# Filters moved within SBUF, and GpSimd's tables at later slots, in a Fourier filter with an MLP behind it

## Chip, core and metric

The kernel runs on one core of one Trainium2 chip. The metric is the device time of one execution in microseconds (us); the kernel before takes 736.68 us, the median of three runs (736.36 to 736.72). Engines are named as in the profile: PE is TensorE's matmul, PEld its weight load, DVE is VectorE, ACT is ScalarE, POOL is GpSimd and SP is SyncE, which here only issues DMAs.

## The reference

Eight batches of 3008 rows and 256 channels go through a global filter in the frequency domain, and each row of the result through a two-layer MLP with an exact GELU:

```python
def _attn_ref(x, filt_r, filt_i):           # x: 8 x 3008 x 256; filters: 1505 x 256
    X = np.fft.rfft(x, axis=1)
    F = (filt_r + 1j * filt_i)[None, :, :]
    return np.fft.irfft(X * F, n=x.shape[1], axis=1)

def _moe_ref(x, w_in, w_out):               # x: 24064 x 256; w_in: 256 x 2048; w_out: 2048 x 256
    h = x @ w_in
    g = 0.5 * h * (1.0 + erf(h / sqrt(2)))
    return g @ w_out
```

The output is 24064 x 256 in float32.

## The kernel before

**The transform.** A batch's 3008 rows are split as 47 x 64, so that the Fourier transform becomes two stages of small matmuls with a table of twiddle factors between them, the product with the filters, and two stages back. For batches 1 to 7 the stages have these names. `fold` (line 102) makes sums and differences of the two halves of x in place, on DVE; `s1` (line 418) is the first stage, in four calls c = 0 to 3 of eight matmuls, whose results DVE and ACT copy out of PSUM into `a_sb` and SP writes to a DRAM buffer R1. `r1` reads that back in another order as `b_sb`. `s2` (line 451) is the second stage, in three units u; `s2_out` multiplies its results by the filters on DVE, and `s2_sum` adds the parts of the complex product (L477, L478). `s3` is the first stage back; its results go through `v_sb` to a DRAM buffer R2, `r2` reads them as `d_sb`, and `s4` is the last stage, which uses the table T4a and writes the ring `y_sb` that the MLP reads. Batch 0 goes through a path of its own (`c1` to `c4`), which uses the filters F as they were loaded.

**The filters.** `F` holds the filters for 24 frequencies k on 64 partitions, loaded in three pieces (k from 0, 4 and 12) by POOL's DMA queue; `dup_filters` copies them to the other 64 partitions. Later batches need the same filters in another order, `Fu`: 128 partitions and six columns m, two for each unit. In the kernel before, `save_filters` writes F to DRAM (16 DMAs on SP), and `load_filters_again` reads it back into Fu, which lies over one half of F: columns m = 0 and 1 by POOL's queue at slot 1, and columns 2 to 5 by SP's at slot 18.

**The tables.** POOL builds what batches 1 to 7 need beside the filters: `table_2_parities` (T2p, read by s2), `table_u_pick` (for `table_u`, which makes the table U that s3 reads), `table_4_rows` and `weights_4` (T1g, T2g and two columns of weights), from which `table_4_factors` makes the factors of T4a with three matmuls and three copies on ACT, and `table_4_all`, which builds T4a of products of these factors in eight parts, two to a call; a part is two products (L414) and a sum (L416). T2, the table that several of these read, shares its buffer with the tile `s_sb` of the MLP.

**The MLP.** Rows are taken in 47 tiles of 512. A tile t has 16 slots, one for each 128 columns of the hidden layer: `mm1` (L643) gives 128 x 512 to a bank of PSUM, ACT applies the GELU (L646) and writes `g_sb`. The second matmul of all tiles but two uses seven products in place of eight (`mm2_seven`, L719), of sums that DVE makes: `sums_1` (L688), `sums_2` (L694) and `sums_3` (L701, into the tile `s4_sb`). Tiles 0 and 2 use the plain product (L659).

**What sets the order.** There is no scheduler: the order of each engine's instructions is the order in which the program is written. A loop runs over slots s = 0 to 767, 16 for each tile; `put(slot, f, ...)` lists a call for a slot, and at each slot the listed calls come first, then this slot's share of the second matmul and its mm1. The calls of batch b + 1 are so spread over the slots of batch b's rows. An instruction waits for what it reads and for the buffer that it writes, and all behind it on its engine or DMA queue waits with it. `gate` (line 143) is a copy of one element on POOL: what is behind it in POOL's queue waits until that element is written. `evac` copies out of PSUM, on ACT when told "act" and on DVE when told False.

Of the kernel before, what the change touches and what calls it, by code (L numbers as in the profile page):

```python
# [20 lines left out]
HB = 32  # L21
# [10 lines left out]
class _Mix:  # L32
    def __init__(self, ctx, tc, x, filt_r, filt_i, w_in, w_out, out):
        self.tc, self.nc = tc, tc.nc
        self.x, self.filt_r, self.filt_i = x, filt_r, filt_i
        self.w_in, self.w_out, self.out = w_in, w_out, out
        self.B, self.S, self.D = x.shape
        self.DFF = w_in.shape[1]
        assert self.S == NA * NB and self.D == 256 and self.DFF == 2048
        pool = lambda name, bufs, **kw: ctx.enter_context(tc.tile_pool(name=name, bufs=bufs, **kw))  # L40
        P = bass.MemoryType.PSUM
        self.const = pool("const", 1)
        self.px = pool("px", 1)
        self.pa = pool("pa", 3)
        self.pb = pool("pb", 2)
        self.pp = pool("pp", 3)
        self.pv = pool("pv", 2)
        self.pd = pool("pd", 3)
        self.pool = pool
        self.po = pool("po", 4)  # L50
        self.py = pool("py", 1)
        self.pg = pool("pg", 2)
        self.pq = pool("pq", 1)
        self.small = pool("small", 1)
        self.dram = pool("dram", 2, space=bass.MemoryType.DRAM)
        c = self.const
        self.T1 = c.tile([2 * NA, 96], BF16, name="T1")
        self.T2p = c.tile([128, K1, 2, 2, 16], BF16, name="T2p")
        self.xs = c.tile([128, 4, 256], BF16, name="xs")
        self.U = c.tile([128, 2, 2 * HB], BF16, name="U")  # L60
        self.T4a = c.tile([96, HB, 96], BF16, name="T4a")
        self.T4c = c.tile([96, NA, 2], BF16, name="T4c")
        self.F = c.tile([128, 2, K1, 256], BF16, name="F")
        self.Fu = self.F[:, 0].rearrange("p (t a m) c -> p t a m c", t=2, a=2)
        self.w_in_sb = c.tile([128, 2, self.DFF], BF16, name="w_in_sb")
        self.w_out_sb = c.tile([128, 16, self.D], FP16, name="w_out_sb")
        self.w_sums = c.tile([128, 4, 8, 128], FP16, name="w_sums")
        self.ps, self.st = {}, {}
        self.flip = 0
# [46 lines left out]
            for q, a in enumerate((direct, mirror)):  # L116
                nc.gpsimd.dma_start(out=self.F[32 * q:32 * q + 32, t, k0:k0 + k, :], in_=a)

    def save_filters(self, k0, k):

        if "Fd" not in self.st:
            self.st["Fd"] = self.dram.tile([2, 2, 4, 2, 16, 6, 256], BF16, tag="Fd", name="Fd")
        for t in range(2):
            for q in range(2):
                for c in range(k0 // 6, (k0 + k) // 6):
                    o = self.st["Fd"][:, t, c, q].rearrange("a i m c -> i a (m c)")
                    if q:
                        o = o[:, ::-1]
                    self.nc.sync.dma_start(out=o, in_=self.F[32 * q:32 * q + 32, t, 6 * c:6 * c + 6, :])

    def load_filters_again(self, eng, m0, m):

        for t in range(2):
            for a in range(2):
                i = self.st["Fd"][a, t, :, :, :, m0:m0 + m, :].rearrange("c q i m d -> (c q i) (m d)")
                eng.dma_start(out=self.Fu[:, t, a, m0:m0 + m, :].rearrange("p m d -> p (m d)"), in_=i)

    def dup_filters(self, eng, k0, k):
        for k in range(k0, k0 + k, 2):
# [278 lines left out]
    def s1(self, b, c):  # L418

        nc = self.nc  # L420
        if c == 0:
            self.st[b, "R1"] = self.dram.tile([NB, 48, 256], BF16, tag="R1", name="R1")
        if b == 1 and c == 3:
            at = self.pp.tile([128, 2, 4, 256], BF16, tag="p12", name="p12").rearrange("p t k c -> p (t k) c")
        else:
            at = self.pa.tile([128, 8, 256], BF16, tag="a", name="a_sb")
        x = self.st[b, "s", c], self.st["x1"][:, 1, 4 * c:4 * c + 4]
        lent = "o" if b == 1 and c < 2 else "h"
        ps = [[self.bank("ps_s1", lent if i == v == 0 else "f") for v in range(2)] for i in range(2)]
        for i in range(2):  # L430
            for d in range(2):
                for v in range(2):
                    nc.tensor.matmul(ps[i][v][64 * d:64 * d + 64, :], lhsT=self.T1s[64 * v:64 * v + NA],  # L433
                                     rhs=x[d][64 * v:64 * v + NA, 2 * i:2 * i + 2, :], start=True, stop=True)
# [59 lines left out]
        self.s3_out(b, u, 0)  # L494

    def s3_out(self, b, u, i):
        vt = self.pv.tile([128, 2, 512], BF16, tag="v", name="v_sb")
        for c in range(2):
            self._evac(vt[:, c], self.st[b, "ps3"][2 * i + c], False if b == u == i == c == 1 else "act")
        for a in range(2):  # L500
            self.nc.sync.dma_start(out=self.st[b, "R2"][:, u, a, 2 * i:2 * i + 2],
                                   in_=vt[64 * a:64 * a + 64].rearrange("p c (m d) -> p c m d", m=2))
# [191 lines left out]
        self.nc.vector.tensor_tensor(out=a21[:, k], in0=self.st["s", t][:, k, 0], in1=a22[:, k], op=ALU.add)  # L694

    def sums_3(self, t, i):
        if i == 0:
            self.st["s4", t] = self.pq.tile([128, 8, 256], FP16, tag="s4", name="s4_sb")
        _, a12, s2, _ = self.quarters(t)
        k = slice(i, i + 4)  # L700
        self.nc.vector.tensor_tensor(out=self.st["s4", t][:, k], in0=a12[:, k], in1=s2[:, k], op=ALU.subtract)  # L701

    def mm2_seven(self, t, lo, hi):

        nc, v = self.nc, self.nc.vector.tensor_tensor
        a11, a12, s2, a22 = self.quarters(t)
        w = self.w_out_sb.rearrange("p (i k) (n o) -> p k n i o", k=2, n=2)
        q = self.w_sums
        s31, s4 = self.st["s", t], self.st.get(("s4", t))
        ops = ((a11, w[:, 0, 0]), (a12, w[:, 1, 0]), (s2, q[:, 1]), (s31[:, :, 0], q[:, 2]),  # L710
               (s31[:, :, 1], q[:, 0]), (a22, q[:, 3]), (s4, w[:, 1, 1]))
        last = t == self.B * self.S // TCH - 1
        for n in range(lo, hi):
# [4 lines left out]
            a, b = ops[m]  # L718
# [69 lines left out]
def kernel(  # L788
# [14 lines left out]
    g = m.small  # L803
# [58 lines left out]
    m.warm_up(1)  # L862
    m.c1t(0, (False, act))
    m.dup_filters(nc.gpsimd, 4, 20)
    for k in (12, 0):
        m.save_filters(k, 12)
    m.c1t(1, (act,))
    m.table_3_copy(1, 0)
    m.c2(0)
# [46 lines left out]
    def put(slot, f, *a):  # L916
        at.setdefault(slot, []).append((f, a))
# [5 lines left out]
    for b in range(1, B):  # L923
        hi = first(b)
        e = 4 * (b == B - 1)
        s1, n1, r1 = (4, 2.75, 16) if b == 1 else (hi - 87, 3.7, hi - 73) if b == 2 else (hi - 94 - e, 3.7, hi - 80 - e)
        s2 = (30, 43, 56) if b == 1 else (hi - 74, hi - 59, hi - 44) if e else (hi - 64 + (b == 2), hi - 48, hi - 32)
        busy.update(range(s1 - 1, s1 + int(3 * n1) + 2))
        for c in range(4):
            slot = s1 + int(c * n1 + (b == 1 and c in (1, 2)))  # L930
            put((0, 1, 5, 8)[c] if b == 1 else (70, 74, 86, 94)[c] if b == 2 else hi - 94 - (20, 13, 8, 6)[c], m.fold, b, c)
            put(slot, m.s1, b, c)
        for u in range(3):
# [16 lines left out]
    for b in range(1, B):  # L950
# [8 lines left out]
        for u in range(7, -1, -1):  # L959
            due = (b * S + GRP * u) // TCH * 16  # L960
            end = min(end, due - 2 if u or b > 1 else 83)
            if b == u == 1:
                end = 85
            for half in (1, 0):
                while end in busy:
                    end -= 1
                assert end > after[b] + 7
                put(end, m.s4, b, u, half, act if half or end in crowd or b == 1 and u == 0 else False)
                busy.add(end)
                end -= 1 if u < 3 else 2  # L970
            if u % 2 == 0:
                put(after[b] if u == 0 else end - 11, m.r2, b, u // 2)

    put(0, m.table_4_rows, g)
    put(0, m.weights_4, g)
    put(0, m.table_u_pick, g)
    put(0, m.table_2_parities)
    put(14, m.table_4_factors, g)
    put(18, m.table_u)
    parts = [(w, h) for w in range(0, HB, 8) for h in range(2)]  # L980
    for i, slot in enumerate((15, 45, 52, 104)):
        put(slot, m.table_4_all, parts[2 * i:2 * i + 2])
    put(1, m.load_filters_again, nc.gpsimd, 0, 2)
    put(18, m.load_filters_again, nc.sync, 2, 4)
    put(20, m.weight_sums)
    plain = (0, 2)
    seven = [t for t in range(NT) if t not in plain]
# [54 lines left out]
```

## Time and profile before

| | us |
|---|---|
| median of three runs | 736.68 |
| the profiled execution | 737.13 |
| its span | 735.3 |
| PE busy in the span | 716.1 |
| first matmul of the MLP (slot 0) | 38.24 |
| first s2 of batch 1 (slot 30) | 62.90 |
| first s4 of batch 1 (slot 82) | 112.67 |

A profile is one execution of the program as the hardware profiler recorded it, with times in us from the start of the span. A line of the timeline gives start, length, engine, source line and operation, the tile written and the tiles read, the shape and how often; brackets at its end hold the time for which the engine was idle before it, and the instruction that ended this. Lines of the windows view give a stretch's length and how long each engine was busy in it. The TensorE clock is at its full rate in every slice of this profile. The start of the span, to 38 us, is batch 0's transform; from there PE works on the MLP with the transforms of the later batches in between.

### The profile page before, as it was taken

The numbers are of one execution on the slowest core, as the hardware profiler recorded it, in microseconds if no ns is written. First come the engines' busy times: TensorE is split into PE (matmuls) and PEld (weight loads), VectorE is DVE, ScalarE is ACT, GpSimd is POOL, SyncE is SP. The second block draws the span as 40 slices with busy tenths as digits, with TensorE's granted clock in tenths as the row PEclk, the third lists the DMA queues.
The fourth block names the chain that finished last, engine by engine and source line by source line (L and its number), as shares of the span: only waits on it lengthen the run. The fifth ranks groups of instructions, "written<-read, shape, count | busy, mean of one in ns | idle before, by whom it ended". The sixth has DMA issues, their size and how long they took to land.

```text
span 735.3 us, 22145 instructions
## 1 busy us (share of the span) xinstructions
PE 716.1 (97%) x9063; PEld 506.5 (69%) x9213; DVE 604.6 (82%) x1105; ACT 575.4 (78%) x1049; POOL 291.2 (40%) x547
## 2 busy tenths in 40 slices
PE   8999999999999999999999999999999999999998
PEld 4856666677777767676677767666677767777776
DVE  8886797899887998789986989779998898675566
ACT  6997677688887888778887788877888788777773
POOL 7895744656122553134621355114631122122121
PEclk9999999999999999999999999999999999999999
DMA  8996435655345643545545455455544433311011
GB/s 145 211 187 213 107 91 116 196 144 110 83 132 172 125 99 105 149 145 117 119 124 171 104 115 124 116 151 132 120 109 127 148 100 102 111 38 52 30 58 59
DMA packets 81190, 89.30 MB, mean 121 GB/s; under 512 B 13201, under 2 KB 60433, under 8 KB 81089
## 3 DMA queue, kind: packets, MB, share of 16 engines
q0 software_dynamic: 22480, 40.02, 23.8%
q1 hardware_dynamic: 58193, 47.66, 23.4%
q8 instruction: 72, 1.18, 0.7%
q14 instruction: 29, 0.24, 0.1%
q10 hardware_dynamic: 416, 0.20, 0.1%
HBM read 55.57 MB, written 48.23 MB: 141 GB/s over the span
## 4 chain that ended last, share of the span: by engine, by line
PE 88%; DVE 3%; DMA 3%; POOL 2%; issue 2%; ACT 1%; DVEq 0%; POOLq 0%
PE ps_o L719 40%; PE ps_h L643 38%; PE ps_s L518 3%; DMA x_sb<-in_x_dram 2%; PE ps_o L659 2%; PE ps_s L433 2%; PE ps_s L491 2%; PE ps_s L460 2%; DMA F<-in_filt_i_dram 1%; ACT g_sb L646 1%; DVE g_sb L694 1%; POOL F L141 1%; DVE s_sb L688 1%; DVE a_sb L331 1%; POOL x_sb L90 0%
## 5 line engine op out<-in xcount | busy, mean ns | idle before, releaser
L646 ACT ACTIVATE g_sb<-ps_h 128x512 f16<-128x512 f32 x752 | 445.7, 603 | 138.8 <-PE ps_h L643 114.9
L643 PE MATMUL ps_h<-y_sb,w_in_sb 128*128 128x512 bf16 (+3 forms) x1454 | 414.2, 365 | 0.6
L766 POOL DMA_DIRECT2D out_dram<-ost x231 | 131.7, 577 | 380.5 <-DVE ost L748 370.0
L719 PEld LDWEIGHTS <-g_sb 128*128 128x128 f16 x2880 | 188.9, 98 | 84.4 <-issue 14.4
L719 PEld LDWEIGHTS <-s_sb 128*128 128x128 f16 x2160 | 145.3, 98 | 53.4 <-issue 3.1
L643 PEld LDWEIGHTS <-w_in_sb 128*128 128x128 bf16 x1600 | 125.7, 98 | 7.6 <-issue 1.3
L719 PE MATMUL ps_o<-w_sums,g_sb 128*128 128x128 f16 x1440 | 124.9, 219 | 2.4 <-DVE g_sb L694 0.9
L719 PE MATMUL ps_o<-w_sums,s_sb 128*128 128x128 f16 x1440 | 123.3, 219 | 1.9 <-DVE t_sb L734 0.2
L688 DVE TENSOR_TENSOR s_sb<-g_sb 128x1024 f16<-128x1024 f16 x180 | 119.2, 693 | 0.7 <-ACT g_sb L646 0.6
L719 PE MATMUL ps_o<-w_out_sb,g_sb 128*128 128x128 f16 x1440 | 116.4, 219 | 1.8
L471 DVE TENSOR_TENSOR p<-ps_s,F 128x1024 bf16<-128x1024 f32 x84 | 101.9, 1217 | 9.4 <-PE ps_s L460 8.0
L99 POOL DMA_DIRECT2D x_sb<-in_x_dram x156 | 79.4, 516 | 2.8 <-DMA x_sb<-in_x_dram 1.0
L694 DVE TENSOR_TENSOR g_sb<-s_sb,g_sb 128x1024 f16<-128x1024 f16 x90 | 63.7, 708 | 1.5
L719 PE MATMUL ps_o<-w_out_sb,s_sb 128*128 128x128 f16 x720 | 62.5, 219 | 0.9
L701 DVE TENSOR_TENSOR s_sb<-g_sb 128x1024 f16<-128x1024 f16 x90 | 61.5, 684 | 0.0
L741 DVE TENSOR_TENSOR t_sb<-t_sb,ps_o 128x256 f32<-128x256 f32 x45 | 18.8, 417 | 39.8 <-PE ps_o L719 39.3
L518 PEld LDWEIGHTS <-d_sb 96*128 96x128 bf16 x448 | 31.3, 97 | 26.0 <-issue 1.3
L329 ACT ACTIVATE y_sb<-ps_s 128x376 bf16<-128x376 f32 x95 | 45.5, 479 | 3.1 <-PE ps_s L518 3.1
L329 ACT ACTIVATE v_sb<-ps_s 128x512 bf16<-128x512 f32 x83 | 45.5, 608 | 1.5 <-PE ps_s L491 1.3
L748 DVE TENSOR_TENSOR ost<-t_sb,ps_o 128x256 f32<-128x256 f32 x88 | 32.9, 415 | 13.9 <-PE ps_o L719 13.8
L331 DVE CAST a_sb<-ps_s 128x512 bf16<-128x512 f32 x54 | 34.7, 684 | 11.6 <-PE ps_s L433 11.4
L736 DVE TENSOR_TENSOR ost<-t_sb,ps_o 128x256 f32<-128x256 f32 x45 | 18.6, 414 | 25.8 <-PE ps_o L719 25.8
(157 smaller groups left out, 563.5 us busy)
## 6 DMA issues: line engine op xcount, KB each, us to landing
out_dram<-ost POOLq DMA_DIRECT2D x127, 128.0 KB, 2.7
b_sb<-R SPq DMA_DIRECT2D x21, 512.0 KB, 4.6
R<-v_sb SPq DMA_DIRECT2D x84, 128.0 KB, 2.4
d_sb<-R SPq DMA_DIRECT2D x56, 192.0 KB, 4.1
R<-a_sb SPq DMA_DIRECT2D x108, 96.0 KB, 2.2
x_sb<-in_x_dram POOLq DMA_DIRECT2D x48, 94.0 KB, 2.8
x_sb<-in_x_dram POOLq DMA_DIRECT2D x48, 48.0 KB, 2.7
x_sb<-in_x_dram POOLq DMA_DIRECT2D x12, 188.0 KB, 5.3
```

Source lines behind the costliest of these rows:

```text
L99: self.nc.gpsimd.dma_start(out=xt[64 * v + to:64 * v + to + m, h, 4 * c:4 * c + 4 * n, :], in_=xv[h][at:at + m, w:w + 4 * n, :])
L329: self.nc.scalar.activation(out=out, in_=in_, func=AF.Copy, scale=1.0 if scale is None else scale)
L331: self.nc.vector.tensor_copy(out=out, in_=in_)
L471: v(out=w[:, a], in0=ps.unsqueeze(2).to_broadcast([128, 2, 2, 256]), in1=f.unsqueeze(1).to_broadcast([128, 2, 2, 256]), op=ALU.mult)
L518: nc.tensor.matmul(ps[:, 94 * i:94 * i + 94], lhsT=d[:, (grp % 2) * 4 + i, 128 * half:128 * half + 128], rhs=self.T4a[:, 4 * grp + i, 0:2 ...
L643: nc.tensor.matmul(ps[:, o:o + n], lhsT=w[:, dc], rhs=self.ring[:, dc, off:off + n], start=(dc == 0), stop=(dc == 1))
L646: nc.scalar.activation(out=self.st["g", t][:, jc, :], in_=ps, func=AF.Gelu)
L688: self.nc.vector.tensor_tensor(out=self.st["s", t][:, i:i + 2], in0=a, in1=b, op=ALU.subtract)
L694: self.nc.vector.tensor_tensor(out=a21[:, k], in0=self.st["s", t][:, k, 0], in1=a22[:, k], op=ALU.add)
L701: self.nc.vector.tensor_tensor(out=self.st["s4", t][:, k], in0=a12[:, k], in1=s2[:, k], op=ALU.subtract)
L719: nc.tensor.matmul(ps[:, (m + 1) % 2, sub, :], lhsT=a[:, i, 128 * sub:128 * sub + 128], rhs=b[:, i], start=i == 0, stop=i == 7)
L766: eng.dma_start(out=out, in_=tile_[lo - r0:lo - r0 + n])
```

## The change

Five things are changed together.

1. Later batches' filters. `save_filters` and `load_filters_again` go. `move_filters(m0, m)` copies from F to Fu by DMAs on SP, from SBUF to SBUF, and Fu is a buffer of its own. Each DMA takes every second partition of 32 (16 partitions), both of the filters' parts t and m columns; for c = 0 of the second call the two parts go separately. `move_filters(0, 2)` has 16 DMAs and stands where the stores stood; `move_filters(2, 4)` has 20 and stands at slot 18.
2. Room. The space of F, once moved, is used for `s4_sb`, for the two `v_sb` buffers and for T4a; their pools go.
3. Tables. The calls of slot 0 go to slot 9, behind a gate on the last element that fold 3 of batch 1 writes, with table_2_parities first. `table_u` goes from slot 18 to 24, `table_4_factors` from 14 to 38. The four calls of `table_4_all` go from slots 15, 45, 52 and 104 to 47, 54, 101 and 114, the third behind a gate on batch 2's last `a_sb`.
4. Batch 1's calls. s1 goes from slots 4, 7, 10, 12 to 4, 8, 11, 13; r1 from 16 to 17; the units' s2 from 30, 43, 56 to 30, 44, 58, with what hangs on them, so s3 from 41, 54, 67 to 41, 55, 69 and r2 of group 0 from 71 to 73. The slots of s4 stay.
5. One copy out of PSUM: that of s4 of batch 1, group 1, half 0, goes from DVE to ACT.

```diff
-        self.T4a = c.tile([96, HB, 96], BF16, name="T4a")
-        self.Fu = self.F[:, 0].rearrange("p (t a m) c -> p t a m c", t=2, a=2)
+        self.Fu = c.tile([128, 2, 2, 6, 256], BF16, name="Fu")
+        f = self.F.rearrange("p t k c -> p (t k c)")
+        self.s4_sb = f[:, 0:2048].bitcast(FP16).rearrange("p (i n) -> p i n", i=8)
+        self.v_sb = [f[:, o:o + 1024].rearrange("p (c d) -> p c d", c=2) for o in (2048, 3072)]
+        self.T4a = f[0:96, 4096:7168].rearrange("p (w m) -> p w m", w=HB)
...
-    def save_filters(self, k0, k):
-        if "Fd" not in self.st:
-            self.st["Fd"] = self.dram.tile([2, 2, 4, 2, 16, 6, 256], BF16, tag="Fd", name="Fd")
-        for t in range(2):
+    def move_filters(self, m0, m):
+        for c in range(4):
             for q in range(2):
...
-    def load_filters_again(self, eng, m0, m):
-        for t in range(2):
-            for a in range(2):
-                i = self.st["Fd"][a, t, :, :, :, m0:m0 + m, :].rearrange("c q i m d -> (c q i) (m d)")
-                eng.dma_start(out=self.Fu[:, t, a, m0:m0 + m, :].rearrange("p m d -> p (m d)"), in_=i)
+                for e in range(2):
+                    o, k = 32 * c + 16 * q, 6 * c + m0
+                    for t in ((0, 1),) if c or m0 == 0 else ((0,), (1,)):
+                        t = slice(t[0], t[-1] + 1)
+                        i = self.F[32 * q + e:32 * q + 32:2, t, k:k + m, :]
+                        self.nc.sync.dma_start(
+                            out=self.Fu[o:o + 16, t, e ^ q, m0:m0 + m, :].rearrange("p t m c -> p t (m c)"),
+                            in_=i.rearrange("p t m c -> p t (m c)"))
...
-    for k in (12, 0):
-        m.save_filters(k, 12)
+    m.move_filters(0, 2)
...
-        s1, n1, r1 = (4, 2.75, 16) if b == 1 else ...
-        s2 = (30, 43, 56) if b == 1 else ...
+        s1, n1, r1 = (4, 3.3, 17) if b == 1 else ...
+        s2 = (30, 44, 58) if b == 1 else ...
...
-            slot = s1 + int(c * n1 + (b == 1 and c in (1, 2)))
+            slot = (4, 8, 11, 13)[c] if b == 1 else s1 + int(c * n1)
...
-                put(end, m.s4, b, u, half, act if half or end in crowd or b == 1 and u == 0 else False)
+                put(end, m.s4, b, u, half, act if half or end in crowd or b == 1 and u < 2 else False)
...
-    put(0, m.table_4_rows, g)
-    put(0, m.weights_4, g)
-    put(0, m.table_u_pick, g)
-    put(0, m.table_2_parities)
-    put(14, m.table_4_factors, g)
-    put(18, m.table_u)
+    put(9, lambda: m.gate(m.st["x1"][0:1, 1, 15, 0:1]))
+    put(9, m.table_2_parities)
+    put(9, m.table_u_pick, g)
+    put(9, m.table_4_rows, g)
+    put(9, m.weights_4, g)
+    put(24, m.table_u)
+    put(38, m.table_4_factors, g)
+    put(101, lambda: m.gate(m.st[2, "a"][0:1, 3, 0:1]))
     parts = [(w, h) for w in range(0, HB, 8) for h in range(2)]
-    for i, slot in enumerate((15, 45, 52, 104)):
+    for i, slot in enumerate((47, 54, 101, 114)):
         put(slot, m.table_4_all, parts[2 * i:2 * i + 2])
-    put(1, m.load_filters_again, nc.gpsimd, 0, 2)
-    put(18, m.load_filters_again, nc.sync, 2, 4)
+    put(18, m.move_filters, 2, 4)
```

More of the change, by code (lines that the diff above doesn't have):

```diff
@@ L46, in __init__ @@
         self.pp = pool("pp", 3)
-        self.pv = pool("pv", 2)
         self.pd = pool("pd", 3)
@@ L117, in load_filters @@
                 nc.gpsimd.dma_start(out=self.F[32 * q:32 * q + 32, t, k0:k0 + k, :], in_=a)
-    def save_filters(self, k0, k):
-        if "Fd" not in self.st:
-            self.st["Fd"] = self.dram.tile([2, 2, 4, 2, 16, 6, 256], BF16, tag="Fd", name="Fd")
-        for t in range(2):
+    def move_filters(self, m0, m):
+        for c in range(4):
             for q in range(2):
[L125 to L129, printed above, removed]
-    def load_filters_again(self, eng, m0, m):
-        for t in range(2):
-            for a in range(2):
-                i = self.st["Fd"][a, t, :, :, :, m0:m0 + m, :].rearrange("c q i m d -> (c q i) (m d)")
-                eng.dma_start(out=self.Fu[:, t, a, m0:m0 + m, :].rearrange("p m d -> p (m d)"), in_=i)
+                for e in range(2):
[6 more added lines that the diff above has]
+                            in_=i.rearrange("p t m c -> p t (m c)"))
     def dup_filters(self, eng, k0, k):
@@ L426, in s1 @@
             at = self.pa.tile([128, 8, 256], BF16, tag="a", name="a_sb")
+        self.st[b, "a"] = at
         x = self.st[b, "s", c], self.st["x1"][:, 1, 4 * c:4 * c + 4]
@@ L496, in s3_out @@
     def s3_out(self, b, u, i):
-        vt = self.pv.tile([128, 2, 512], BF16, tag="v", name="v_sb")
+        vt = self.v_sb[i]
         for c in range(2):
@@ L696, in sums_3 @@
     def sums_3(self, t, i):
-        if i == 0:
-            self.st["s4", t] = self.pq.tile([128, 8, 256], FP16, tag="s4", name="s4_sb")
         _, a12, s2, _ = self.quarters(t)
         k = slice(i, i + 4)
-        self.nc.vector.tensor_tensor(out=self.st["s4", t][:, k], in0=a12[:, k], in1=s2[:, k], op=ALU.subtract)
+        self.nc.vector.tensor_tensor(out=self.s4_sb[:, k], in0=a12[:, k], in1=s2[:, k], op=ALU.subtract)
     def mm2_seven(self, t, lo, hi):
@@ L708, in mm2_seven @@
         q = self.w_sums
-        s31, s4 = self.st["s", t], self.st.get(("s4", t))
+        s31, s4 = self.st["s", t], self.s4_sb
         ops = ((a11, w[:, 0, 0]), (a12, w[:, 1, 0]), (s2, q[:, 1]), (s31[:, :, 0], q[:, 2]),
@@ L925 @@
         e = 4 * (b == B - 1)
-        s1, n1, r1 = (4, 2.75, 16) if b == 1 else (hi - 87, 3.7, hi - 73) if b == 2 else (hi - 94 - e, 3.7, hi - 80 - e)
-        s2 = (30, 43, 56) if b == 1 else (hi - 74, hi - 59, hi - 44) if e else (hi - 64 + (b == 2), hi - 48, hi - 32)
+        s1, n1, r1 = (4, 3.3, 17) if b == 1 else (hi - 87, 3.7, hi - 73) if b == 2 else (hi - 94 - e, 3.7, hi - 80 - e)
+        s2 = (30, 44, 58) if b == 1 else (hi - 74, hi - 59, hi - 44) if e else (hi - 64 + (b == 2), hi - 48, hi - 32)
         busy.update(range(s1 - 1, s1 + int(3 * n1) + 2))
         for c in range(4):
-            slot = s1 + int(c * n1 + (b == 1 and c in (1, 2)))
+            slot = (4, 8, 11, 13)[c] if b == 1 else s1 + int(c * n1)
             put((0, 1, 5, 8)[c] if b == 1 else (70, 74, 86, 94)[c] if b == 2 else hi - 94 - (20, 13, 8, 6)[c], m.fold, b, c)
```

## The prediction

> **What bounds the kernel.** I read the busy table first, then the busy time by stage, then the timeline of the stages in which TensorE is not full, then the DMA queues.
>
> ```profile
> PE 716.1 (97%) x9063; PEld 506.5 (69%) x9213; DVE 604.6 (82%) x1105; ACT 575.4 (78%) x1049; POOL 291.2 (40%) x547
> ```
>
> TensorE (PE) is busy 716.1 of 735.3 us; the change neither adds nor removes any of its work, apart from where it waits. So what can be won is idle PE time, and the stages say where it lies (columns: stage; its length; busy us and instructions of PE, PEld, DVE, ACT, POOL; PE clock; DMA share; GB/s):
>
> ```profile
> 38.20:50.10 11.90, 10.93 (x78) 4.97 (x77) 11.10 (x19) 11.18 (x23) 11.30 (x30) 1.00 1.07 204
> 50.10:62.90 12.80, 12.60 (x84) 7.86 (x85) 5.86 (x7) 10.64 (x21) 11.84 (x15) 1.00 0.79 264
> 62.90:72.50 9.60, 9.31 (x118) 6.23 (x120) 9.09 (x13) 6.46 (x11) 2.12 (x6) 1.00 0.40 118
> 72.50:76.20 3.70, 2.76 (x50) 1.58 (x50) 2.24 (x6) 2.23 (x5) 1.27 (x3) 1.00 0.56 88
> 76.20:80.00 3.80, 3.48 (x60) 2.23 (x61) 3.26 (x5) 2.60 (x5) 1.70 (x4) 1.00 0.61 137
> 80.00:112.00 32.00, 31.63 (x364) 21.83 (x370) 27.42 (x44) 23.90 (x42) 21.56 (x35) 1.00 0.40 99
> 130.00:134.50 4.50, 3.72 (x43) 2.16 (x42) 4.46 (x6) 2.93 (x7) 4.33 (x6) 1.00 0.86 239
> ```
>
> From 80 to 112 us PE is idle 0.37 us in 32, about 0.01 us per us: that is the floor. Above it lie 0.97 us in 38.2 to 50.1 (batch 1's first stage, s1), 0.94 and 0.32 us in 72.5 to 80 (batch 1's units 0 and 1), and 0.78 us in 130 to 134.5 (batch 2's s1). These 3.0 us, and PE work moved into such a gap, are nearly all that the change can win; everything from 160 us on is the same program.
>
> **Term 1, the s1 slots.** The timeline of PE in the first of these stages (start, length, what, and the idle time before with its releaser):
>
> ```profile
> 40.76 1.47 PE L643 MATMUL ps_h<-y_sb,w_in_sb 128*128 128x512 bf16 x6
> 42.16 1.16 PE L433 MATMUL ps_s<-x_sb,T1s 47*64 47x512 bf16 x8
> 43.25 1.47 PE L643 MATMUL ps_h<-y_sb,w_in_sb 128*128 128x512 bf16 x6
> 44.98 0.59 PE L433 MATMUL ps_s<-x_sb,T1s 47*64 47x512 bf16 x5 [0.26 <-ACT g_sb L646]
> 45.94 0.41 PE L433 MATMUL ps_s<-x_sb,T1s 47*64 47x512 bf16 x3 [0.37 <-DVE a_sb L331]
> ```
>
> The first s1 goes from 40.11 to the next matmul at 40.76, 0.65 us. The second takes 42.16 to 43.25 (1.09), the third about 44.72 to 46.28 (1.56), the fourth about 47.81 to 48.80 (1.0): 1.7 us over three times 0.65. They wait for their PSUM banks, which VectorE (DVE) empties; DVE is busy 11.10 of 11.90 us there, with folds of 0.69 and evictions of 0.64 us that the change leaves alone. So the fourth s1 still ends near 48.8, but s1 calls 1 to 3 come one slot later, and PE will have done one slot more by then: four 256-column and two 512-column matmuls, which take 0.87 us from slot to slot (49.25 to 50.12). ScalarE (ACT) bounds the gain: its idle time up to 51.3 us is about 1.0. I take **-0.9** (ends -1.0 and 0, if ACT binds).
>
> That the tables run behind the folds adds nothing to this. The folds take 0.68 to 0.72 us with GpSimd (POOL) beside them and 0.61 to 0.69 later without. What waits on the moved tables: POOL starts them when fold 3 is done, near 47.2, and by their present lengths they end in this order: T2p 5.6 us (52.8), pick 2.6 (55.4), T1g and T2g 3.3 (58.7), weights 3.0 (61.7). T2p is read at slot 30 (62.9 us now), pick by the U table at slot 24 (near 58), T1g at slot 38 (near 70): all covered, pick by some 2 us. T2 shares its buffer with the s tile of sums_1, which DVE starts at 59.6 now; if POOL is 2 us late, the 1.86 us that DVE waits at 63.38 covers it, and what goes past it delays unit 0 one for one.
>
> **Term 2, the factors.** table_4_factors stands at slot 14: from 50.12 to 51.37 PE needs 1.25 us for a slot that takes 0.87 beside it. At slot 38 it falls right ahead of unit 0's s3, where PE waits for DVE anyway (0.42 and 0.87 us at 72.6 and 73.9), so its 0.4 us hide: **-0.4** (ends -0.4 and +0.3, if ACT's three evictions of 0.29 us hold up a bank).
>
> **Term 3, unit spacing.** Unit 1's s2 starts two slots behind unit 0's s3, and waits 0.22 us for ACT's v_sb and 0.2 us more; with s2 at 44 (and 58, three slots behind s3 at 55) one slot of cover is added. The s4 eviction of unit group 1 that goes from DVE (0.54) to ACT (0.48) helps DVE near 114, where PE waits 0.38 us for L694. Together **-0.3** (ends -0.6 and +0.2, if s4 starts to wait: batch 1's d_sb lands at 108.75 and is read at 112.67; s3 two slots later eats 1.9 of those 3.9 us).
>
> **Term 4, filters.** Removed: 16 stores on SP (0.59 us each, 96 KB, in program order ahead of the s1 stores) and 8 reloads, four on POOL (0.56 each, 53.8 to 56.1) and four on SP (0.47 each). Added on SP: 16 moves of 32 KB in the same place, and 20 (16 of them in twos, 64 KB, c = 0 split) at slot 18. The bytes beside the last filter load fall from 384 KB to 256 KB. That load releases POOL's copies at 22.61:
>
> ```profile
> 22.61 5.96 POOL L141 COPY F<-F 64x1024 bf16<-64x1024 bf16 x6 [0.89 <-DMA F<-in_filt_i_dram]
> 23.68 5.75 DVE L572 TENSOR_TENSOR p<-ps_c,F 128x1024 bf16<-128x1024 f32 x5 [0.26 <-POOL F L141]
> ```
>
> DVE then waited only 0.26 us, so an earlier landing wins at most that: **-0.2** (ends -0.26 and +0.6, if the 128 KB of moves that can now start earlier hold it up). The 20 moves at slot 18 start behind r1's loads, at 56.15. At 0.55 us each and 2.4 us to landing they are in at 69.6. Queued behind them on SP are tile 0's five output stores and r1 of unit 2 (issued 66.55 now, near 71 then); its reader is s2 at slot 58, near 90, and the output tiles have four buffers. First readers and overwriters of F: s4 near 70 (needs the first 8 moves, 60.6 + 2.4), ACT's v_sb at 74.56, unit 1's product at 76.70, T4a after that. Cost **0**; if the cover goes, see the second rival.
>
> **Term 5, T4a's parts beside DVE.** The row that matters most:
>
> ```profile
> 130.67 2.62 DVE L694 TENSOR_TENSOR g_sb<-s_sb,g_sb 128x1024 f16<-128x1024 f16 x1
> 131.11 1.61 POOL L414 TENSOR_TENSOR tmp_sb<-t_sb 96x376 f32<-96x376 f32 x2
> 133.34 0.51 PE L719 MATMUL ps_o<-w_sums,g_sb 128*128 128x128 f16 x6 [0.72 <-DVE g_sb L694]
> ```
>
> A 0.69 us addition took 2.62 while POOL built a part of T4a, and PE waited 0.72. With the gate behind batch 2's last a_sb this pair of parts starts after 133: **-0.7** (ends -0.74 and 0). But the first pair leaves 56 to 62, where DVE is half idle, and the last one goes to slot 114, near 147.4 when POOL has issued its stores, in the midst of unit 0 of batch 2. There DVE has no gap:
>
> ```profile
> 148.48 0.68 DVE L701 TENSOR_TENSOR s_sb<-g_sb 128x1024 f16<-128x1024 f16 x1
> 152.13 0.68 DVE L701 TENSOR_TENSOR s_sb<-g_sb 128x1024 f16<-128x1024 f16 x1
> 153.74 0.41 DVE L478 TENSOR_TENSOR p<-p 128x512 bf16<-128x512 bf16 x1
> 154.82 0.64 PE L491 MATMUL ps_s<-p,U 32*64 32x256 bf16 x32
> ```
>
> s3 at 154.82 follows L478 (done 154.15) by 0.67 us. Elsewhere two parts cost DVE 0.6 (two L688 at 59.6, 1.91 us for 1.28), 1.3 (L477 and L478 at 83 to 85, 2.12 for 0.83), 1.3 (L688 at 93.3) and 2.1 (131). The middle, 1.3, less 0.67 of slack is **+0.5** (ends 0 and +1.5). The two pairs at 47 and 54 lie where pairs lie now.
>
> The GPSIMD Engine Reference of the Trainium skill (section 8, Key points) says that GpSimd shares its SBUF interfaces with VectorE and contends with Vector instructions in a two-port mode or with two SBUF inputs. This speaks against the change: folds and sums all have two SBUF inputs, so by it the tables cost DVE wherever they lie, and +0.5 would be nearer +1.5. The rows agree for sums beside T4a and disagree for folds beside the small tables, 0.72 at most; the rows decide.
>
> **Sum.** -0.9 - 0.4 - 0.3 - 0.2 - 0.7 + 0.5 = -2.0 us. On the profiled execution (737.13 us, of which 735.3 are the span) that is 735.1; its 0.45 above the median of 736.68 is common to both kernels, so I put it at **734.7**. Its own range, half the terms failing or all going full, is 733.4 to 735.8.
>
> **Rivals.** (1) The gains are absorbed: ACT, busy 11.18 of 11.90 us, is the bound in the s1 stage (term 1 nothing), and the T4a pair moved from 131 is paid again at 147 (term 5 nothing). Left are -0.4 - 0.3 - 0.2: **735.8**. For it: ACT's share; against: its waits for PE at 47.4 and 48.2.
> (2) The moves come late on SP. The 16 stores took 18.9 to 31.9, 0.81 us each with waits, and 6.3 us to landing in a full DMA stage. At that price 20 moves end at 56.15 + 16.2 + 6.3 = 78.7, 2.0 us after unit 1's product starts to need them: **736.7**. Against it: the DMA share there is 0.79 now and loses 512 KB.
> (3) Slower: POOL's last T4a pair holds DVE in batch 2's unit 0 twice, each time as at 130.67 (1.93 us): 3.9 less 0.67 is 3.2 in place of 0.5, and the sum is +0.7; with the pair at slot 101, now over L701 and the last a_sb evictions, costing another 1.9 it is +2.6: **739.3**. It decides from the point where the two pairs cost DVE more than 3.2 us, the 2.5 of the other terms and the 0.67 of slack. Against it: two pairs on end have cost 2.6 us (83 and 93) without PE idling.
>
> **How the numbers follow.** Forecast 0.52, rival 1 0.22, rival 2 0.10, rival 3 0.16. About 0.2% (1.5 us) can't be told from no change. Faster holds the forecast and a little of rival 1: 0.57. Same: the rest of rival 1 and rival 2, 0.27. Slower: 0.16. The range goes from all gains in full and nothing lost at 147 (-3.0), with the 0.42 us that DVE idles ahead of fold 2 at 43.27, where x lands late and a DMA stage with fewer bytes could help (733.3), to short of rival 3's full price (737.8).
>
> **What would show it.** Right: s1 calls 2 to 4 under 0.9 us each; no long L694 near 131; slot 14 as short as its neighbours; the Fu moves landed before 76. Wrong: DVE sums over 1.5 us near 147 to 153 with PE idle before L491; SP still issuing moves at 72; DVE idle before L688 near 59 because of T2g.

## The result and the profile after

The changed kernel takes 738.95 us (median of 10 runs, 737.84 to 739.72), the kernel before beside it 737.01 (10 runs, 736.36 to 738.27): a ratio of 1.0025, 95% interval 1.0015 to 1.0035. It is slower by a quarter of a percent, where 734.7 was forecast with a range of 733.3 to 737.8. The profiled execution took 738.78 us, 1.65 more than that of before.

As the two programs do the same MLP slots in the same order, the best first view is the start of the GELU of each slot (slot 0 is ScalarE's first GELU) in both traces. The difference is a running account of what has been won and lost:

| slot | before, us | after − before, us | what happened since the row above |
|---|---|---|---|
| 0 | 38.94 | +0.82 | the start is later |
| 16 | 53.52 | −0.65 | batch 1's s1 and the factors: 1.47 won |
| 44 | 79.36 | −1.36 | unit 1's s2: 0.71 won |
| 64 | 98.14 | −1.55 | 0.19 won |
| 72 | 105.55 | +0.47 | unit 2's s3: **2.02 lost** |
| 84 | 120.92 | +0.47 | nothing |
| 88 | 122.83 | +1.79 | **1.32 lost** |
| 104 | 136.79 | +0.91 | batch 2's s1: 0.89 won |
| 160 | 188.63 | +0.91 | nothing, with the last T4a pair in it |
| 751 | 725.82 | +0.92 | nothing |

Behind the last slot 0.74 us are added: from the last matmul to the end of the span 3.4 us (3.0 before), and from the span to the time measured 2.1 (1.8 before). So the prediction's gains are there, nearly 3.3 us of them, and 5 us of losses beside them. The profile's busy line of the changed kernel, and its busy time by stage (columns as in the prediction):

```profile
PE 723.3 (98%) x9213; PEld 506.1 (69%) x9213; DVE 602.8 (82%) x1105; ACT 575.6 (78%) x1049; POOL 285.9 (39%) x545
38.20:50.10 11.90, 11.46 (x94) 5.18 (x92) 11.10 (x19) 11.63 (x26) 3.26 (x9) 1.00 0.98 193
72.50:76.20 3.70, 2.93 (x43) 1.93 (x42) 1.98 (x5) 2.48 (x6) 0.93 (x2) 1.00 0.89 174
80.00:112.00 32.00, 30.34 (x346) 20.30 (x345) 27.53 (x42) 22.57 (x41) 19.37 (x27) 1.00 0.37 93
112.00:130.00 18.00, 16.49 (x188) 10.37 (x186) 12.99 (x25) 12.86 (x27) 10.41 (x21) 1.00 0.56 117
130.00:134.50 4.50, 4.50 (x52) 2.80 (x51) 4.46 (x9) 3.88 (x9) 2.87 (x5) 1.00 0.62 168
```

PE idles 0.44 us in the s1 stage (0.97 before) and none from 130 to 134.5 (0.78 before): those are the gains. From 80 to 112 it idles 1.66 (0.37 before), and from 112 to 130 1.51 (0.37 before): those are the losses. The first line also corrects the prediction's "floor". PE's records are 9213 here, as many as PEld's; in the trace of before they were 9063, and the 150 that are missing looked like idle time. From 160 to 400 us, where the two programs are alike, PE is busy 239.93 of 240 us with 3158 records here, and was 237.21 with 3108 before. There is no floor of 0.01 us per us.

**The start.** The timeline of SP and POOL (start, length, engine, line and operation), first of the kernel before:

```profile
18.95 12.93 SPq L129 DMA_DIRECT2D Fd<-F  x16
...
17.73 3.98 POOL L141 COPY F<-F 64x1024 bf16<-64x1024 bf16 x4 [0.96 <-DMA F<-in_filt_i_dram]
```

and of the changed kernel:

```profile
13.46 15.26 SPq L130 DMA_DIRECT2D Fu<-F  x16
...
18.90 3.98 POOL L137 COPY F<-F 64x1024 bf16<-64x1024 bf16 x4 [2.17 <-DMA F<-in_filt_i_dram]
23.08 5.95 POOL L137 COPY F<-F 64x1024 bf16<-64x1024 bf16 x6 [0.20 <-DMA F<-in_filt_i_dram]
```

The moves begin at 13.46, while the second and third filter loads are under way; before, SP's stores began at 18.95, as the first of them needed the third piece of F (k from 12). POOL waits for the second load until 18.90 (17.73 before), and starts the last copies at 23.08 (22.61).

**Unit 2's s3.** The timeline of DVE and PE around it, first of the kernel before:

```profile
99.36 0.41 DVE L477 TENSOR_TENSOR p<-p 128x512 bf16<-128x512 bf16 x1
99.70 0.41 DVE L478 TENSOR_TENSOR p<-p 128x512 bf16<-128x512 bf16 x1
100.03 0.68 DVE L688 TENSOR_TENSOR s_sb<-g_sb 128x1024 f16<-128x1024 f16 x1
...
99.69 0.78 PE L491 MATMUL ps_s<-p,U 32*64 32x256 bf16 x32
```

and of the changed kernel, in which L474 is the old L477, L685 the old L688, L691 the old L694 and L488 the old L491:

```profile
99.82 0.68 DVE L685 TENSOR_TENSOR s_sb<-g_sb 128x1024 f16<-128x1024 f16 x1
100.53 0.69 DVE L691 TENSOR_TENSOR g_sb<-s_sb,g_sb 128x1024 f16<-128x1024 f16 x1
101.14 0.42 DVE L729 COPY t_sb<-ps_o 128x256 f32<-128x256 f32 x1
101.47 0.42 DVE L474 TENSOR_TENSOR p<-p 128x512 bf16<-128x512 bf16 x1
...
99.99 0.42 PE L488 MATMUL ps_s<-p,U 32*64 32x256 bf16 x16
101.94 0.65 PE L488 MATMUL ps_s<-p,U 32*64 32x256 bf16 x16 [1.52 <-DVE p L474]
```

Every operation shown has its old duration. (A pair of T4a parts on POOL costs DVE 1.3 us a little earlier, from 90 to 96 us, but it did so before too.) But the unit comes two slots later, and so the last sum that s3 needs was written behind the next tile's sums_1, sums_2 and a copy: 0.68 + 0.69 + 0.42 us of work in front of it on an engine that has no gap there. PE waits 1.52 us in the middle of s3.

**Slots 84 to 88.** The timeline some 10 to 20 us later, first of POOL in the kernel before:

```profile
108.75 0.47 POOL L146 COPY gate<-d_sb 1x1 bf16<-1x1 bf16 x1 [7.86 <-DMA d_sb<-R]
...
112.49 2.88 POOL L766 DMA_DIRECT2D out_dram<-ost  x5
```

and of POOL, DVE and PE of the changed kernel:

```profile
112.23 0.18 POOL L142 COPY gate<-d_sb 1x1 bf16<-1x1 bf16 x1 [12.38 <-DMA d_sb<-R]
...
116.26 2.89 POOL L761 DMA_DIRECT2D out_dram<-ost  x5
...
119.67 0.42 DVE L737 TENSOR_TENSOR ost<-t_sb,ps_o 128x256 f32<-128x256 f32 x1 [1.71 <-DMA out_dram<-ost]
...
123.01 1.02 PE L640 MATMUL ps_h<-y_sb,w_in_sb 128*128 128x512 bf16 x4 [1.25 <-DVE a_sb L327]
```

The late s3 makes d_sb late. POOL's queue has a gate on d_sb, which opens at 112.23 (108.75 before). Behind the gate stand loads of x and then the stores of a finished output tile, which go out at 116.26 (112.49 before). With four output buffers, DVE can't write the next tile until a store has landed; it waits 1.71 us, its evictions of `a_sb` come late, and PE waits 1.25 us for them.

### The profile page after: what moved, and what is told of

It is laid out like the page before. It is cut to its first block, busy times and chain, and to the rows that moved or that the text cites. A ratio compares the mean times of both kernels' runs of the same rounds, so it can differ in the third digit from the quotient of the medians.

```text
span 736.7 us, 22328 instructions
## 1 busy us (share of the span) xinstructions
PE 723.3 (98%) x9213; PEld 506.1 (69%) x9213; DVE 602.8 (82%) x1105; ACT 575.6 (78%) x1049; POOL 285.9 (39%) x545
## 4 chain that ended last, share of the span: by engine, by line
PE 87%; POOL 4%; DMA 3%; issue 3%; DVE 3%; ACT 1%; SPq 0%; DVEq 0%; POOLq 0%
PE ps_h L640 40%; PE ps_o L714 36%; PE ps_s L515 3%; PE ps_s L430 2%; PE ps_s L488 1%; DMA b_sb<-R 1%; PE ps_s L457 1%; POOL tmp_sb L410 1%; POOL out_dram L761 1%; DMA x_sb<-in_x_dram 1%; PE ps_c L587 1%; ACT y_sb L325 1%; POOL x_sb L101 1%; PE ps_o L656 1%; PE ps_c L565 0%
## 5 line engine op out<-in xcount | busy, mean ns | idle before, releaser
L640 PE MATMUL ps_h<-y_sb,w_in_sb 128*128 128x512 bf16 (+3 forms) x1600 | 445.4, 366 | 1.5 <-DVE a_sb L327 1.2
L714 PEld LDWEIGHTS <-s_sb 128*128 128x128 f16 x1440 | 97.0, 98 | 37.5 <-issue 2.1
L685 DVE TENSOR_TENSOR s_sb<-g_sb 128x1024 f16<-128x1024 f16 x180 | 118.6, 690 | 0.7 <-ACT g_sb L643 0.6
L468 DVE TENSOR_TENSOR p<-ps_s,Fu 128x1024 bf16<-128x1024 f32 x84 | 101.9, 1217 | 8.9 <-PE ps_s L457 7.3
L691 DVE TENSOR_TENSOR g_sb<-s_sb,g_sb 128x1024 f16<-128x1024 f16 x90 | 61.7, 687 | 1.5
L696 DVE TENSOR_TENSOR F<-g_sb 128x1024 f16<-128x1024 f16 x90 | 62.8, 697 | 0.0
L714 PE MATMUL ps_o<-w_out_sb,F 128*128 128x128 f16 x720 | 62.5, 219 | 0.0
L714 PEld LDWEIGHTS <-F 128*128 128x128 f16 x720 | 48.3, 98 | 16.0 <-issue 0.8
L325 ACT ACTIVATE F<-ps_s 128x512 bf16<-128x512 f32 x83 | 45.5, 608 | 3.3 <-PE ps_s L488 3.2
L743 DVE TENSOR_TENSOR ost<-t_sb,ps_o 128x256 f32<-128x256 f32 x88 | 32.9, 415 | 14.0 <-PE ps_o L714 14.0
```

The source lines that it names most:

```text
L325: self.nc.scalar.activation(out=out, in_=in_, func=AF.Copy, scale=1.0 if scale is None else scale)
L468: v(out=w[:, a], in0=ps.unsqueeze(2).to_broadcast([128, 2, 2, 256]), in1=f.unsqueeze(1).to_broadcast([128, 2, 2, 256]), op=ALU.mult)
L640: nc.tensor.matmul(ps[:, o:o + n], lhsT=w[:, dc], rhs=self.ring[:, dc, off:off + n], start=(dc == 0), stop=(dc == 1))
L685: self.nc.vector.tensor_tensor(out=self.st["s", t][:, i:i + 2], in0=a, in1=b, op=ALU.subtract)
L696: self.nc.vector.tensor_tensor(out=self.s4_sb[:, k], in0=a12[:, k], in1=s2[:, k], op=ALU.subtract)
L714: nc.tensor.matmul(ps[:, (m + 1) % 2, sub, :], lhsT=a[:, i, 128 * sub:128 * sub + 128], rhs=b[:, i], start=i == 0, stop=i == 7)
```

## The experiments

Two theories for the middle losses stood against each other: **A**, the two slots by which unit 2 was moved cause both; and a rival, that DVE is slowed there by the tables. For the start, **C**: the moves run beside the last filter loads. All times below are medians, and each ratio is to the kernel before, run beside it on the same chip: at 737.32 beside experiments 1 to 4, 737.44 beside 5 to 8 and 737.58 beside 9 and 10.

**1. The order of the first moves.**

```diff
-        for c in range(4):
+        for c in (2, 3, 0, 1) if m0 == 0 else range(4):
```

> The changed kernel with the first 16 moves in the order c = 2, 3, 0, 1, so that none starts before the last piece of the filters has landed (in the changed kernel the first starts at 13.46 us, and slot 0's GELU starts at 39.76 for 38.94 before). Theory C (early moves share the DMA engines with the filter loads, and POOL's copies of F start 1.2 us late, at 18.90): POOL's first copy back at 17.7, slot 0 at 38.7 to 39.0, about 0.8 us off the time, 738.1. Rival (the late start has another cause, such as the moves' landing or chance): slot 0 stays at 39.6 or later and the time at 738.9.

Measured: 739.28 us, ratio 1.0024 (1.0012 to 1.0035), so nothing won in the time. In its trace the moves begin at 21.38, POOL's copies at 17.81 and 22.39, and slot 0 is at 38.73, 1.03 us earlier than in the changed kernel. One trace each would not do, as slot 0 differs by 0.95 us among the five traces with this part of the program as in the changed kernel. But all twelve traces of this study agree: with early moves the third filter load lands at 22.8 to 23.7 us and slot 0 is at 39.26 to 40.21; in the seven others the load lands at 21.9 to 22.7 and slot 0 is at 38.61 to 39.16. Theory C holds for the start. At slot 16 only 0.42 us are left, as PE then waits 0.64 us for w_out:

```profile
45.07 0.60 PE L656 MATMUL ps_o<-w_out_sb,g_sb 128*128 128x256 f16 x4 [0.64 <-DMA w_out_sb<-in_moe_w_out_dram]
```

The middle losses are all there. So in this pair of traces an early start is worth less than half of itself: the next thing that is late is a load. Even the 0.42 is not sure: two traces with early moves (experiments 3 and 4) stand as far ahead at slot 16 as this one.

**2. Unit 2 back at its slot.**

```diff
-        s2 = (30, 44, 58) if b == 1 else ...
+        s2 = (30, 44, 56) if b == 1 else ...
```

> The changed kernel with unit 2's s2 of batch 1 back at slot 56 (s3 at 67, r2 at 71). Theory A (VectorE is the bound from 89 to 107 us; the later s2 starts its chain later, PE gives back 1.8 us at unit 2's s3, d_sb lands 3.5 us later, POOL's queue waits for it, the output stores behind it go out late and DVE waits 1.71 us for an output buffer, 1.3 us of PE): both losses go, PE's lag between slots 66 and 90 loses about 3 us, 736.0. Theory B (the pair of T4a parts at slot 54 is what makes DVE late): the pair stays where it is, so at most the 1.3 us behind d_sb go, 737.6.

Measured: 736.32 us, ratio 0.9990 (0.9982 to 0.9999). The sums are in the old order again, s3 runs without a wait, and POOL's gate opens at 108.29:

```profile
99.08 0.64 PE L488 MATMUL ps_s<-p,U 32*64 32x256 bf16 x32
...
108.29 0.18 POOL L142 COPY gate<-d_sb 1x1 bf16<-1x1 bf16 x1 [8.27 <-DMA d_sb<-R]
```

By slot 88 it is 2.55 us ahead of the changed kernel. One number, 58 to 56, undoes both losses, more than theory B allowed with its pair left in place: theory A is shown. Something else is lost for it. From slot 44 to 72 this kernel gives back 0.66 us of the 0.71 that the later unit 1 had won (so do experiments 6 and 10), as unit 2's s2 now stands one slot behind unit 1's s3, where it stood two behind before, and waits for an eviction in its middle. The timeline of PE, first before, then here:

```profile
89.35 0.82 PE L460 MATMUL ps_s<-b_sb,T2p 64*32 64x256 bf16 x32
...
87.94 0.71 PE L457 MATMUL ps_s<-b_sb,T2p 64*32 64x256 bf16 x16
88.96 0.67 PE L457 MATMUL ps_s<-b_sb,T2p 64*32 64x256 bf16 x16 [0.31 <-DVE F L327]
```

**3. Five output buffers.**

```diff
-        self.po = pool("po", 4)
+        self.po = pool("po", 5)
```

> The changed kernel with five output buffers in place of four. If the 1.3 us between slots 84 and 86 come from DVE's wait for an output buffer whose store stands behind the gate on d_sb in POOL's queue: that wait (1.71 us at 119.67) is gone, about 1.3 us off the time, 737.6. If they come from x arriving late for the folds, or from POOL itself: nothing changes, 738.9. The loss at slots 66 to 72 stays in both cases.

Measured: 738.02 us, ratio 1.0011 (1.0002 to 1.0020). The loss between slots 84 and 88 is gone (+1.55 us against before at both, where the changed kernel goes from +0.47 to +1.79), the wait of 1.52 us at s3 is there as in the changed kernel: the second loss goes by way of the output buffers. From slot 64 to 72 this trace loses 3.53 us where the changed kernel lost 2.02; the last section says why.

**4. A T4a pair away from DVE's full stretch.** The second call of table_4_all at slot 72 in place of 54:

```diff
-    for i, slot in enumerate((47, 54, 101, 114)):
+    for i, slot in enumerate((47, 72, 101, 114)):
```

> The changed kernel with the second call of table_4_all at slot 72 in place of 54, so that POOL builds nothing beside unit 2's products (90 to 96 us). Theory B (the pair makes DVE late): DVE gains 1.3 us ahead of the sums, s3's wait of 1.52 us falls to about 0.3, and with it 1.2 to 2 us of the time, 737.2. Theory A (the late start of the chain alone): DVE still gains the 1.3 us of the pair's price there, but pays it again near 106 to 112; the time falls by less than 0.6 us.

Measured: 743.26 us, ratio 1.0084 (1.0071 to 1.0097), which neither theory expected. POOL, free by 97.72, reached the call while DVE was still at the sums of slots 66 to 72, as the timeline of DVE and POOL shows:

```profile
97.31 2.32 DVE L474 TENSOR_TENSOR p<-p 128x512 bf16<-128x512 bf16 x1
99.55 1.20 DVE L475 TENSOR_TENSOR p<-p 128x512 bf16<-128x512 bf16 x1
...
97.72 1.62 POOL L410 TENSOR_TENSOR tmp_sb<-t_sb 96x376 f32<-96x376 f32 x2
```

A sum of 0.41 us takes 2.32, its neighbour 1.20, and the three large ones behind it 1.30, 1.20 and 0.86 in place of 0.68, 0.69 and 0.42: 4.3 us in all for one pair of parts, where pairs elsewhere cost 0.6 to 2.1. As a test of the rival it says no more than that DVE is the bound at this place; how long s3 would wait without a pair near it stays open. As a price it is the dearest one of this study. The page GPSIMD Engine Reference of the Trainium skill (section 8, Key points), which the prediction weighed, is borne out by these rows for sums with two SBUF inputs.

**5. Fillers in the wait.** 14 matmuls of ones between the halves of unit 2's s3, written to a bank that s3 fills afterwards, to see whether the wait also costs clock.

```diff
+            for i in range(14 if b == 1 and u == 2 and m == 1 else 0):
+                nc.tensor.matmul(ps[0][:, 256:512], lhsT=self.ones[:, 0:128], rhs=self.ones[:, 0:256], start=True, stop=True)
```

> The changed kernel with 14 matmuls of ones between the two halves of unit 2's s3 of batch 1, into the half of a bank that the second half of s3 then overwrites: 14 times 0.107 us, 1.5 us, in which PE waited 1.52 us for DVE. Theory D (where PE waits there, its clock drops to half for 3.4 us in a part of the executions, as the profiles of the kernels with five output buffers and with the table call at slot 72 show at 102.25 and 101.69 us; that is the spread of the changed kernel's times and most of what it loses): every run has a mean clock of 0.999 or more, the spread falls below 1.5 us and the median falls by 0.7 to 1.5 us, though the wait in the profile is as long. Rival (the spread is DMA timing): clock and median stay, 738.9, or get worse by what the fillers overhang.

Measured: 738.91 us, ratio 1.0021 (1.0012 to 1.0031). All 12 runs had a mean clock of 0.999 or more, against 6 of 10 of the changed kernel: the clock went as theory D said. The time did not. The ratio is 0.3 us better than the changed kernel's, well inside the intervals, the fall of 0.7 to 1.5 us did not come, and the spread stayed at 2.4 us. The fillers are hardly to blame, as the second half of s3 starts 0.10 us after DVE's sum is done (0.05 without them). The profiled execution is a late one (740.07 us): its slot 0 is 0.45 us later than the changed kernel's, and the sums beside the T4a pair took 2.63 us for 2.06. The last section comes back to the clock.

**6. Both corrections**, 1 and 2 together.

> The changed kernel with both the moves' order c = 2, 3, 0, 1 and unit 2 at slot 56. If the two effects are independent: slot 0 near 38.7, a lag against the kernel before of about -2.0 us at the end, 735.9, 0.2% under the kernel before. If the later moves cost as much in the s1 stage as they win at the start (they did 0.6 of 1.03 us): 736.3, as with unit 2 alone.

Measured: 736.01 us, ratio 0.9983 (0.9974 to 0.9992). It has the lowest median of all kernels run, and is faster than the kernel before; its profiled span is 733.8 us against 735.3. Slot 0 is at 39.16 and the lead at the end 1.94 us, close to the 2.0 of independent effects. But from experiment 2 alone (0.9990) its ratio can't be told apart.

**7. The gate alone**, put into the kernel before, whose last table call stands at slot 104 anyway:

```diff
+        self.st[b, "a"] = at
...
+    put(104, lambda: m.gate(m.st[2, "a"][0:1, 3, 0:1]))
```

> The kernel before with a gate on batch 2's last a_sb ahead of the last call of table_4_all, at slot 104; nothing else. The prediction's term 5: the L694 of 2.62 us at 130.67 falls to 0.7, the lag falls by 0.7 to 0.9 us between slots 100 and 104 and the time with it, 736.4. Rival (DVE pays the pair's price later): the lag comes back after slot 104, 737.3.

Measured: 736.25 us, ratio 0.9985 (0.9977 to 0.9994). The long sum is gone from DVE's timeline, and POOL's pair comes behind the gate:

```profile
131.35 0.69 DVE L695 TENSOR_TENSOR g_sb<-s_sb,g_sb 128x1024 f16<-128x1024 f16 x1
...
133.71 0.51 POOL L146 COPY gate<-a_sb 1x1 bf16<-1x1 bf16 x1 [1.94 <-DVE a_sb L331]
```

Between slots 100 and 104 it wins 0.90 us on before, kept to the end. This one gate comes to nearly as much as experiment 6.

**8. The s1 slots alone**, in the kernel before:

```diff
-        s1, n1, r1 = (4, 2.75, 16) if b == 1 else ...
+        s1, n1, r1 = (4, 3.3, 17) if b == 1 else ...
...
-            slot = s1 + int(c * n1 + (b == 1 and c in (1, 2)))
+            slot = (4, 8, 11, 13)[c] if b == 1 else s1 + int(c * n1)
```

> The kernel before with s1 of batch 1 at slots 4, 8, 11, 13 and r1 at 17 alone; tables, filters and units as before. The prediction's term 1: 0.9 us of lag won between slots 8 and 14, by the slots alone; the changed kernel won 1.6 there. If all 1.6 come, the slots did it; if 0.9 or less, the moved tables or the smaller traffic beside the x loads gave the rest. The time falls to 736.0 to 736.5, unless DVE gives it back at unit 0.

Measured: 737.52 us, ratio 1.0001 (0.9991 to 1.0012): nothing, and 0.9 us won lies outside the interval. In its trace it is 0.40 us ahead at slot 12, where one s1 call of 0.65 us is still to come that the kernel before has behind it, and 0.26 behind from slot 14. (A trace alone would show little here: experiment 7 is the kernel before up to slot 104, and stands 0.70 us behind it at slot 16.) What held it first:

```profile
46.01 0.60 PE L659 MATMUL ps_o<-w_out_sb,g_sb 128*128 128x256 f16 x4 [1.34 <-DMA w_out_sb<-in_moe_w_out_dram]
```

With the s1 calls out of the way PE reaches the first second-layer matmul earlier, and waits for its weights.

**9 and 10. The filters through DRAM again**, with all else as in the changed kernel; 10 has unit 2 at slot 56 besides.

```diff
-    m.move_filters(0, 2)
+    for k in (12, 0):
+        m.save_filters(k, 12)
...
-    put(18, m.move_filters, 2, 4)
+    put(18, m.load_filters_again, nc.sync, 0, 2)
+    put(18, m.load_filters_again, nc.sync, 2, 4)
```

> The changed kernel with its filters again through DRAM: the 16 stores where they stood, all 8 reloads on SP at slot 18, into the same separate Fu; tables, slots, gates and room as in the changed kernel. Theory C (the early SBUF moves put the start 0.8 us back, because they run beside the last filter loads): slot 0 back at 38.9 to 39.1 us, against 39.3 to 40.2 in the five kernels that have the moves in their first order. Theory F (the 1.6 us won in slots 8 to 14 came from the lighter DMA traffic, x and w_out landing earlier): they are not won, and slot 14 is within 0.4 us of before. Rival to F (they came from the tables behind the folds and the factors off slot 14, whatever carries the filters): slot 14 is 0.8 us or more earlier than before, as the start no longer loses anything. Under either the 1.8 us at slots 66 to 72 and the 1.3 us at 84 to 88 stay lost.

> As the other run, with unit 2's s2 of batch 1 at slot 56 as before, so that nothing is lost at slots 66 to 72 and 84 to 88. By theory F about 736.3 us (the gate's 0.9 us won, little else, 0.3 outside the span lost); by its rival 735.0 to 735.6, and the best of all.

Measured: 740.20 us, ratio 1.0043 (1.0028 to 1.0058), and 737.21, ratio 0.9995 (0.9986 to 1.0003). Slot 0 is at 39.02 and 38.61: theory C again. On theory F against its rival the two disagree, though they are one program up to slot 55: slot 16 is 0.81 us ahead of before in one and 0.10 in the other. PE waited for w_out in both, the first time for 0.61 us and the second for 1.72:

```profile
45.33 0.60 PE L662 MATMUL ps_o<-w_out_sb,g_sb 128*128 128x256 f16 x4 [0.61 <-DMA w_out_sb<-in_moe_w_out_dram]
...
46.03 0.60 PE L662 MATMUL ps_o<-w_out_sb,g_sb 128*128 128x256 f16 x4 [1.72 <-DMA w_out_sb<-in_moe_w_out_dram]
```

After that both are alike. So the load of w_out is what ends the wait, and its landing differs by 0.7 us from one execution to the next. The rival's fixed gain is not there. Theory F has some support over all twelve traces: the first half of w_out landed by 45.02 us in six of the seven with moves, and at 45.97 to 46.02 in four of the five with stores. That lighter traffic is the reason is not shown. Each of the two still stands worse against the kernel before than its twin with moves: 1.0043 against 1.0025, some 1.3 us, and 0.9995 against 0.9990, some 0.4, with intervals that overlap both times. So no cost of the moves themselves shows on the whole, early start or not. About 0.4 us of the difference lies behind the last slot (PE's end to the measured time: 5.92 and 5.91 us, 5.3 to 5.6 with moves, 4.78 in the kernel before).

## Why the prediction was wrong, point by point

**Terms 1 and 2: right in size, and with the wrong limit.** From slot 0 to 16 the changed kernel needs 13.11 us, the kernel before 14.58: 1.47 won for a forecast of 1.3. The three later s1 calls keep close to the next matmul, as asked:

```profile
43.87 0.63 PE L430 MATMUL ps_s<-x_sb,T1s 47*64 47x512 bf16 x8
44.42 1.04 PE L640 MATMUL ps_h<-y_sb,w_in_sb 128*128 128x512 bf16 x4
```

But the term was bounded by ACT alone. Another limit is w_out's landing, which no row of before showed as a wait, since the s1 calls kept PE busy until it came. In the changed kernel's trace it came at 44.63, in time; that is luck as far as term 1 goes, which did not ask for it. Where it lands at 46.0 the slots win nothing (experiments 8 and 10). Term 2 is right: from slot 13 to 14 every trace with the factors at slot 38 gains 0.38 or 0.39 us on before, experiment 8 with the factors at 14 nothing, and at slot 38 nothing is paid. (The later folds take 0.68 and 0.69 us, not 0.61.)

**Term 3: the step that failed.** It valued the spacing at −0.3 with an end of +0.2 "if s4 starts to wait". The spacing of unit 1 gave 0.71, more than forecast, though experiment 2 shows that 0.66 of it goes again unless unit 2 moves too. But the two slots of unit 2 cost 2.02 and then 1.32. The term looked along one chain, from d_sb's landing to s4, and no wait of s4 is in the trace there. It did not ask in which order DVE's work is written once unit 2 is two slots later, nor what else on POOL stands behind the arrival of d_sb: a gate, and behind the gate the output stores. Experiments 2 and 3 show both. The sign of the whole change turned here. None of the prediction's signs of being wrong came, and all its signs of being right did: no sign watched unit 2.

**Term 4: the wrong end.** "If the 128 KB of moves that can now start earlier hold it up" was the right mechanism and +0.6 its bound; −0.2 was taken. The start lost 0.82 us in this trace, and 0.3 to 1.3 in the other four with this order of moves. Without the early moves (experiment 1) slot 16 comes 0.4 us earlier, which is no more than traces of one program part differ there. At another load the change may have helped: the first half of w_out lands 7.2 us after its issue (8.1 before).

**Term 5: half right.** The pair at 131: forecast −0.7, measured −0.89, and experiment 7 gives it alone, 0.90. The pair near 147 cost 0 for a forecast of +0.5. The contention is there, as the timeline of the changed kernel shows:

```profile
149.39 1.11 DVE L696 TENSOR_TENSOR F<-g_sb 128x1024 f16<-128x1024 f16 x1
...
153.47 1.17 DVE L696 TENSOR_TENSOR F<-g_sb 128x1024 f16<-128x1024 f16 x1
...
155.73 0.64 PE L488 MATMUL ps_s<-p,U 32*64 32x256 bf16 x32
```

Two sums of 0.68 us took 1.11 and 1.17, 0.92 in all, not 1.3, and the slack paid for it: s3 runs in one piece.

**The rivals.** Rival 1 (ACT as the bound) did not come. Rival 2 counted the moves nearly right, and they were harmless:

```profile
55.94 13.97 SPq L130 DMA_DIRECT2D Fu<-F  x20
```

20 moves took 0.70 us each where 0.55 was assumed and 0.81 feared; SP was free at 69.9, the last move landed at 71.6, and no matmul and no DVE operation in the trace waits for Fu. Rival 3 had the right side, and its time of 739.3 is near the 738.95 measured, but for a wrong reason: DVE in batch 2's unit 0 lost nothing. The loss lay on the same engine, 50 us earlier, beside a T4a pair that cost DVE 1.3 us in both kernels and so is not what changed. One small sum of the prediction does not come out: with all gains in full and nothing lost its own range begins at 733.7, not 733.4.

**Left open.** The 0.74 us behind the last matmul: all instructions there are the same, and last as long; the last store lands 2.19 us after PE's end (2.06 before), and the rest lies behind it. Whether SBUF moves that start later keep all of the gain was tried only in the form of experiments 1 and 6.

## What to carry to other kernels

Where an engine's order is the order of the program, moving a call by two slots changes what it stands behind on every engine it uses: write out that engine's new order around the call, and price the wait at the work newly in front of it. Follow a late transfer past its reader, to everything queued behind the gates that wait for it. And ask of a wait that ends what is late next; here, in several traces, a load that no row had shown as a wait set the limit.

## What the runs showed of the hardware

The wait of 1.52 us in s3 can halve the granted clock. In experiment 3's trace it fell to half at 102.25 us for 3.41 us, 0.9 us after the wait had ended, and a pair of matmuls that lasts 0.59 us elsewhere took 1.06:

```profile
102.43 1.06 PE L640 MATMUL ps_h<-y_sb,w_in_sb 128*128 128x512 bf16 x2
```

This fall is the 1.5 us by which that trace lost more from slot 64 to 72 than the changed kernel's, whose own trace has the wait and no fall. In experiment 4's, after a wait of 0.80 us it fell 0.6 us into a second one of 3.26, and stayed at half for 6.83 us. Among the changed kernel's runs, 4 of 10 had a mean clock below 0.999, with a median of 739.54 us against 738.6 of the rest, so this is worth some 0.4 us of the mean. With experiments 1, 3 and 9, which have the same wait, it is 18 runs of 42. In experiments 2, 6 and 10, which don't have the wait, and in 5, which fills it, no run of 46 fell below. The fall does come without it, but seldom: in 1 of 24 runs of experiments 7 and 8, and in 5 of 84 of the kernel before beside the experiments. The page TensorE: Matmul & The Clock Gate of the Trainium skill ("Part 1: The HAM clock gate") puts the fall after at least one idle window of about 3.4 us. The length of the fall in experiment 3 agrees with such a window; the cause does not, as here a wait of 1.52 us amid small matmuls (32 x 64) came before it.
